# One-hot rows moved from GpSimd to ScalarE and VectorE, gathers queued behind masks, first scalings by ScalarE

## The chip, the cores and the metric

The kernel runs on one core of one Trainium2 chip, in one launch. Its engines work from queues of their own and meet at semaphores: TensorE (PE; its weight loads are shown apart as PEld), VectorE (DVE), ScalarE (ACT), GpSimd (POOL) and SyncE (SP), which issues most DMA transfers. Indirect transfers (gathers by a list of rows) are issued by GpSimd. The metric is the device time of one execution in microseconds, lower is better. [...]

## The reference

Three layers follow one another, all in fp32 at the interface. First a gated linear attention over 4 batches, 8 heads, 768 positions, 48 dimensions per head:

```python
for t in range(S):
    state = alpha[:, :, t, :, None] * state + np.einsum('bhd,bhe->bhde', k[:, :, t], v[:, :, t])
    y[:, :, t] = np.einsum('bhd,bhde->bhe', q[:, :, t], state)
```

Its output, as 3072 tokens of 384 values, goes through a mixture of 8 experts with hidden width 1024. A noisy gate takes the two best experts of each token; each token's two expert outputs are weighted by a softmax of the two logits and added:

```python
top2 = np.argpartition(-noisy_logits, 2, axis=1)[:, :2]
...
h = np.maximum(x[mask] @ w1[e], 0.0)
out[mask] += top2_w[mask, k, None] * (h @ w2[e])
```

Last comes a gated layer of width 1536 on all tokens: `(sigmoid(x @ w_gate) * (x @ w_val)) @ w_out`.

## The kernel before

The products of the experts and of the last layer are made from numbers split in a high and a low part, with three matmuls for each product (lines 521 to 523). The high part is a copy by ScalarE, the low part the difference, by an engine that the caller names (`split`, line 466). For weights that is GpSimd (`wlo`, 128x768 at a time, line 469).

**Attention and router rounds** (about the first 150 us). The attention is done in 24 units: 6 chunks of 128 positions, 4 pairs of heads each. `unit(u, ...)` (line 254) writes the order of all engines by hand: scores of unit u+1 (`st_S`, which ends in ScalarE's copy `am` and GpSimd's mask of it, line 115), then outputs of unit u (`st_Y`, ScalarE's `xt`), state update, transposes (`xr`), the state's scaling (`st`), and the scans of unit u+3 on VectorE (`st_T`), with `d`, a small copy by ScalarE, made one unit ahead (`st_D`). Four slots in a unit, TURN, COUNT, DECIDE and LAST, take other steps. After each chunk the gate routes its 512 tokens in a round: logits, softplus, the two best experts, counts, ranks. Then the round writes its tokens in a table, token number by expert and rank, by matmuls with one-hot rows: `ohl` (128 columns for the low seven bits of the rank, times the token number) as weights and `ohh` (56 columns for expert and the rank's high part) as the moving side, four tiles of 128 tokens for each of the two choices (`router_table`, line 408: `hot`, `mm`, `add`). `hot(0)` stands three units after the round's start, `mm(0)` and `hot(1)` in the next unit, `mm(1)` and `add(1)` in the one after (the list `when`, line 971). Rounds 0 to 3 add up in one PSUM tile; that of chunk 3 ends with a copy to `tab`.

**First expert.** The tokens of chunks 0 to 3 that go to expert 0 are gathered early (`early_fetch`: three gathers `xrow` of 128 rows), transposed and used as the first half of expert 0. The rounds of chunks 4 and 5 are worked off beside that half's matmuls; their order from there on is set by the scheduler of the build, which lays out each engine's queue from its own model of times. `ready` (line 1021) then turns the full table into an index, computes the rows and weights for later, and gathers the second half. An expert half is 8 groups of nine or so matmuls (`ph`, then `h` by ScalarE and VectorE) and a row tile's worth of output matmuls each (`py`).

**Second MoE.** Eight blocks of 384 tokens; for each, two rows of every token are gathered (`grow`), the first scaled by its weight on VectorE (line 850, written with a column of zeros), the second scaled and added (line 852), transposed and run through the gated layer: `sg` (line 878) frees the PSUM tiles, `gh` and `gl` are the split of the result. `gl` is made by GpSimd in block 0, by VectorE in the others.

Of the kernel before, what the change touches and what calls it, by code (L numbers as in the profile page):

```python
# [9 lines left out]
FT = mybir.dt.float32  # L10
# [13 lines left out]
def attention(tc, g):  # L24
# [178 lines left out]
    def round_steps(c):  # L203

        v = {}
        hot, mm, add = router_table(tc, g, c)

        def logits():
            v["ls"] = st_L(c)

        def soft():
            v["lt"] = st_P(v["ls"])
            router_soft(tc, g, v)

        def count():
            router_count(tc, g, c, v)

        def rank():
            router_rank(tc, g, c, v)

        fix = [lambda: router_fix(tc, g, v), lambda: router_lack(tc, g, v)] if c == g.c0 else [lambda: None] * 2
        return [logits, soft, lambda: router_choice(tc, g, c, v), count, rank, *fix,
                lambda: hot(0), lambda: mm(0), lambda: (add(0), hot(1)), lambda: mm(1), lambda: add(1)]

    def fill(k):
        for _ in range(k):
# [53 lines left out]
def router_consts(ctx, tc, g):  # L280
# [16 lines left out]
    nc.vector.tensor_scalar(g.tri, g.iotaP, g.tcol, None, op0=OP.is_gt)  # L297
    g.ones = c.tile([128, 128], BF, name="ones")
    nc.vector.memset(g.ones, 1.0)
    g.noise = c.tile([128, g.NT, E], FT, name="noise")  # L300
    g.load_noise = lambda: nc.sync.dma_start(g.noise, g.nh)

    g.mb = [c.tile([128, B + 1, E], BF, name=f"mb{i}") for i in range(2)]
    nc.vector.memset(g.mb[0][:, B], 0.0)
    g.zero = c.tile([128, 1], FT, name="zero")
    nc.vector.memset(g.zero, 0.0)
    g.roff = c.tile([128, E], FT, name="roff")
    nc.vector.memset(g.roff, 0.0)
    g.wts = c.tile([128, g.NT, 2], FT, name="wts")
# [98 lines left out]
def router_table(tc, g, c):  # L408

    nc, rw = tc.nc, g.rw  # L410
    B = g.B
    T = slice(c * B, (c + 1) * B)
    EN = g.E * g.NB
    v = {}

    def hot(k):
        lo = rw.tile([128, B, 128], FR, name="ohl", tag="ohl", bufs=1)
        for b in range(B):
            n = c * B + b
            nc.gpsimd.tensor_scalar(lo[:, b], g.iotaP, g.low[:, n, k:k + 1], g.ids[:, n:n + 1], op0=OP.is_equal, op1=OP.mult)  # L420
        hi = rw.tile([128, B, EN], FR, name="ohh", tag="ohh", bufs=1)
        cf = g.codes.rearrange("p e a -> p (e a)")[:, None, :].to_broadcast([128, B, EN])
        nc.vector.tensor_tensor(hi, cf, g.code[:, T, k:k + 1].to_broadcast([128, B, EN]), op=OP.is_equal)
        v[k] = lo, hi

    def mm(k):
        lo, hi = v[k]
        own = c > g.c0
        tab = v["tab"] = g.pst("tb", [128, EN]) if own else g.ptab
        for b in range(B):  # L430
            nc.tensor.matmul(tab, lo[:, b], hi[:, b], start=b == 0 and (own or c == k == 0), stop=b == B - 1,
                             skip_group_check=True)

    def add(k):

        if c > g.c0:
            nc.vector.tensor_tensor(g.tab, g.tab, v["tab"], op=OP.add)
        elif c == g.c0 and k == 1:
            nc.vector.tensor_copy(g.tab, g.ptab)

    return hot, mm, add


def router_fix(tc, g, v):
# [378 lines left out]
def moe2(tc, g, out):  # L823
# [11 lines left out]
    def load_x(i):  # L835
# [5 lines left out]
        def fetch():  # L841
            for b in range(TB):
                n = i * TB + b
                ga = []
                for k in range(2):
                    r = g.sx.tile([128, g.DM], FT, name="grow", tag="xrow", bufs=5)
                    g.got = nc.gpsimd.indirect_dma_start(out=r, out_offset=None, in_=src, in_offset=bass.IndirectOffsetOnAxis(  # L847
                        ap=g.row[:, n, k:k + 1], axis=0)).ins
                    ga.append(r)
                nc.vector.scalar_tensor_tensor(ga[0], ga[0], g.wts[:, n, 0:1], g.zero.to_broadcast([128, g.DM]),  # L850
                                               op0=OP.mult, op1=OP.add)
                nc.vector.scalar_tensor_tensor(ga[0], ga[1], g.wts[:, n, 1:2], ga[0], op0=OP.mult, op1=OP.add)
                xs.append(ga[0])
            x["h"] = g.sx.tile([128, KD, NT], FR, name="x2h", tag="xh", bufs=2)
            x["l"] = g.sx.tile([128, KD, NT], FR, name="x2l", tag="xl", bufs=2)
# [9 lines left out]
    def compute(i, x, bg, after, before_last=None):  # L865
        xh, xl = x["h"], x["l"]
        gs = []
        for f in range(FB):
# [9 lines left out]
            nc.vector.tensor_tensor(sg, sg, pp[1], op=OP.mult)  # L878
            hh = g.sh2.tile([128, NT], FR, name="gh", tag="h", bufs=26)
            hl = g.sh2.tile([128, NT], FR, name="gl", tag="h", bufs=26)  # L880
            a, b = split(nc, hh, hl, sg, nc.vector if i else nc.gpsimd)
            gs.append((hh, hl))
            with tc.issue_after(a.ins), tc.issue_after(b.ins):
                bg.step(1)
# [23 lines left out]
def kernel(  # L908
# [14 lines left out]
    g = K()  # L923
# [39 lines left out]
    with tc.tile_pool(name="xrp", bufs=1) as g.xr, tc.tile_pool(name="aconst", bufs=1) as g.ac, \  # L963
# [5 lines left out]
        TURN, COUNT, DECIDE, LAST = range(4)  # L969

        when = [(0, COUNT), (1, TURN), (1, DECIDE), (2, COUNT), (2, DECIDE), (3, COUNT), (3, DECIDE), (3, TURN),
                (4, COUNT), (4, DECIDE), (5, COUNT), (5, DECIDE)]
        soon = when[:5] + [(3, LAST)] * 2 + [(4, LAST)] * 5
        late = []
        for c in range(g.NC - 1):
# [9 lines left out]
            first["steps"][0]()  # L985

        u0 = g.c0 * NP + NP + 5
        plan_a[u0][DECIDE].append(early_fetch)
        for d in range(3):
            plan_a[u0 + 2][COUNT].append(lambda d=d: first["steps"][1 + d]())  # L990
        w0 = expert_steps(g, 0, ahead=True)
# [17 lines left out]
    with tc.tile_pool(name="sh", **tile_wise) as g.sh, tc.tile_pool(name="ps2", space=PSUM, **tile_wise) as g.ps2:  # L1009
# [10 lines left out]

        def ready():
            idx = nxt["idx"] = router_index(tc, g)
            router_rows(tc, g, g.rw)
            overflow_plan(tc, g, plan)
            nxt["steps"], nxt["x"] = expert_x(tc, g, 0, *halves[1], g.sx, idx, g.xd)
            nxt["steps"][0]()

        def behind(f):
            with tc.issue_after(g.last_mask), tc.issue_after(g.last_y):
# [125 lines left out]
```

## Time and profile before

| | us |
|---|---|
| median of 3 runs (1123.96 to 1128.1) | 1124.64 |
| the profiled execution | 1121.54 |
| its span, first to last instruction | 1119.8 |
| TensorE busy | 1074.2 (96%) |
| TensorE's weight loads busy | 1032.1 (92%) |
| VectorE busy | 460.3 (41%) |
| ScalarE busy | 374.1 (33%) |
| GpSimd busy | 372.1 (33%) |

The profile shows one execution. Busy shares over the span are means over stages with different limits: TensorE's idle time lies almost all in the first fifth of the span. In the rows below "idle before" is the time in which an engine stood before an instruction, with the instruction that released it. Matmuls are pipelined, so one that follows another overlaps it.

### The profile page before, as it was taken

The page shows a single profiled execution, that of the slowest core. Times are in us where ns is not written, and L with a number is a line of the kernel's source. Part 1 is how long each engine was busy: PE and PEld are TensorE (multiplying, and loading weights), DVE is VectorE, ACT ScalarE, POOL GpSimd, SP SyncE. Part 2 cuts the span into 40 slices and gives each one's busy share as a digit, 9 for nine tenths or more (in the row PEclk, how much of TensorE's full clock was granted, in tenths as well). Part 3 has the DMA queues.
Part 4 walks back from the last instruction along what each step waited for, and adds up shares of the span by engine and source line. Part 5 has one row for each costly group of instructions (what it writes and reads, how often), then busy time and mean ns, then how long its engine had stood idle before and what let it go on. Part 6 is the DMA issues. An engine that isn't in the chain of part 4 may idle for free. (4 is left out here: it accounts for less than half of the span.)

```text
span 1119.8 us, 18728 instructions
## 1 busy us (share of the span) xinstructions
PE 1074.2 (96%) x7618; PEld 1032.1 (92%) x7618; DVE 460.3 (41%) x940; ACT 374.1 (33%) x801; POOL 372.1 (33%) x310
## 2 busy tenths in 40 slices
PE   7889889799999999999999989999999999999998
PEld 6778769699999999999999989999999999999998
DVE  8989834324544354532222432251414141413131
ACT  4646534223333333333333433131313131313131
POOL 4488878523434232324332745220101010100000
PEclk9989879799999999999999999999999999999999
DMA  8766544425646464645332630210101101000000
GB/s 235 198 177 196 140 130 123 132 72 164 209 139 219 144 194 138 198 143 179 90 101 67 187 91 23 79 43 29 32 33 29 36 27 38 22 23 1 22 1 22
DMA packets 48074, 115.50 MB, mean 103 GB/s; under 512 B 6464, under 2 KB 24800, under 8 KB 47984
## 3 DMA queue, kind: packets, MB, share of 16 engines
q1 hardware_dynamic: 41456, 94.60, 27.9%
q0 software_dynamic: 6528, 19.67, 5.9%
q8 instruction: 61, 1.00, 0.4%
q14 instruction: 29, 0.24, 0.1%
HBM read 87.50 MB, written 26.74 MB: 102 GB/s over the span
## 5 line engine op out<-in xcount | busy, mean ns | idle before, releaser
L469 POOL TENSOR_TENSOR wlo<-raw,whi 128x768 fp32r<-128x768 f32 x82 | 151.7, 1856 | 244.3 <-ACT whi L468 244.2
L521 PE MATMUL pg<-x2h,whi 128*128 128x384 f32 x576 | 195.1, 339 | 2.8 <-DVE sg L878 2.8
L523 PE MATMUL pg<-x2h,wlo 128*128 128x384 f32 x576 | 193.4, 336 | 0.0
L522 PE MATMUL pg<-x2l,whi 128*128 128x384 f32 x576 | 193.2, 335 | 0.0
L586 DVE SCALAR_TENSOR_TENSOR h<-ph,h 128x384 fp32r<-128x384 f32 x192 | 78.6, 443 | 200.3 <-ACT h L583 200.3
L878 DVE TENSOR_TENSOR sg<-sg,pg 128x384 f32<-128x384 f32 x96 | 53.1, 553 | 212.4 <-PE pg L523 199.2
L521 PE MATMUL ph<-xh,whi 128*128 128x384 f32 (+1 forms) x384 | 135.6, 354 | 0.6 <-ACT xh L468 0.6
L522 PE MATMUL ph<-xl,whi 128*128 128x384 f32 (+1 forms) x384 | 135.7, 354 | 0.0
L523 PE MATMUL ph<-xh,wlo 128*128 128x384 f32 (+1 forms) x384 | 135.4, 353 | 0.0
L847 POOL DMA_INDIRECT grow<-yd,row x48 | 46.7, 973 | 263.3 <-PE pt L860 197.4
L521 PE MATMUL py<-whi,h 128*128 128x384 f32 x384 | 133.0, 346 | 0.8 <-ACT yrow L609 0.4
L522 PE MATMUL py<-wlo,h 128*128 128x384 f32 x384 | 128.1, 335 | 0.0
L583 ACT ACTIVATE h<-ph 128x448 fp32r<-128x448 f32 (+1 forms) x128 | 65.4, 516 | 177.4 <-PE ph L523 175.1
L523 PE MATMUL py<-whi,h 128*128 128x384 f32 x384 | 118.3, 337 | 1.2 <-DVE h L586 1.1
L521 PEld LDWEIGHTS pg<-x2h,whi 128*128 128x128 f32 x576 | 108.7, 189 | 3.3 <-DVE sg L878 3.1
L522 PEld LDWEIGHTS pg<-x2l,whi 128*128 128x128 f32 x576 | 108.7, 189 | 0.0
L523 PEld LDWEIGHTS pg<-x2h,wlo 128*128 128x128 f32 x576 | 108.6, 189 | 0.0
L521 PE MATMUL po<-whi,gh 128*128 128x384 f32 x288 | 96.3, 334 | 2.1 <-issue 2.1
L468 ACT ACTIVATE gh<-sg 128x384 fp32r<-128x384 f32 x96 | 50.3, 524 | 142.1 <-DVE sg L878 142.0
L523 PE MATMUL po<-whi,gl 128*128 128x384 f32 x288 | 96.2, 334 | 0.0
L522 PE MATMUL po<-wlo,gh 128*128 128x384 f32 x288 | 96.2, 334 | 0.0
L468 ACT ACTIVATE whi<-raw 128x768 fp32r<-128x768 f32 x82 | 68.9, 844 | 67.0 <-DMA raw<-in_w2h_dram 50.6
(169 smaller groups left out, 1770.4 us busy)
## 6 DMA issues: line engine op xcount, KB each, us to landing
ur<-in_uh_dram SPq DMA_DIRECT2D x23, 675.5 KB, 5.6
raw<-in_w1h_dram SPq DMA_DIRECT2D x32, 384.0 KB, 3.6
raw<-in_w2h_dram SPq DMA_DIRECT2D x32, 384.0 KB, 3.9
yd<-yrow SPq DMA_DIRECT2D x48, 192.0 KB, 2.1
w<-t SPq DMA_DIRECT2D x36, 192.0 KB, 2.0
raw<-w SPq DMA_DIRECT2D x18, 384.0 KB, 3.2
xv<-in_vh_dram SPq DMA_DIRECT2D x6, 768.0 KB, 9.0
xd<-xr SPq DMA_DIRECT2D x6, 768.0 KB, 6.1
```

Of the source, the lines that this page charges most:

```text
L468: a = nc.scalar.activation(hi, src, AF.Copy)
L469: b = e.tensor_tensor(lo, src, hi.bitcast(FT), op=OP.subtract)
L521: nc.tensor.matmul(out, wh, mh, start=first, stop=False)
L522: nc.tensor.matmul(out, wh, ml, start=False, stop=False)
L523: nc.tensor.matmul(out, wl, mh, start=False, stop=last)
L583: a = nc.scalar.activation(h[:, :tot], p[:, :tot], AF.Relu)
L586: b = nc.vector.scalar_tensor_tensor(h[:, lo:lo + j - i], p[:, i:j], 0.0, h[:, i:j].bitcast(FT), op0=OP.max, op1=OP.subtract)
L847: g.got = nc.gpsimd.indirect_dma_start(out=r, out_offset=None, in_=src, in_offset=bass.IndirectOffsetOnAxis(ap=g.row[:, n, k:k + 1], axis= ...
L878: nc.vector.tensor_tensor(sg, sg, pp[1], op=OP.mult)
```

## The change

It has five parts.

1. `hot` is split. For the first choice of rounds 0 to 3, ScalarE makes `ohl` tile by tile in two instructions: |low - column|, and then max(0, id - id x that), which is the token number where they agree and 0 elsewhere. The four tiles stand in four slots of one unit. Everywhere else (`hot`) VectorE makes all four tiles of `ohl` in one comparison, without the token number, and ScalarE multiplies the four tiles of `ohh` by it. GpSimd makes none.
2. `early_fetch` moves from the end of one unit to the TURN slot of the next, behind that unit's masks.
3. `ready` gathers directly after the index.
4. The first scaling of gathered rows is ScalarE's in blocks 0 and 1, and a form without the zeros on VectorE in the others.
5. `gl` of block 0 is VectorE's.

```diff
--- before.py
+++ after.py
@@ -203,7 +203,7 @@
     def round_steps(c):
 
         v = {}
-        hot, mm, add = router_table(tc, g, c)
+        hot, part, mm, add = router_table(tc, g, c)
 
         def logits():
             v["ls"] = st_L(c)
@@ -220,7 +220,8 @@
 
         fix = [lambda: router_fix(tc, g, v), lambda: router_lack(tc, g, v)] if c == g.c0 else [lambda: None] * 2
         return [logits, soft, lambda: router_choice(tc, g, c, v), count, rank, *fix,
-                lambda: hot(0), lambda: mm(0), lambda: (add(0), hot(1)), lambda: mm(1), lambda: add(1)]
+                *([lambda b=b: part(0, b) for b in range(B)] if c <= g.c0 else [lambda: hot(0)]),
+                lambda: mm(0), lambda: (add(0), hot(1)), lambda: mm(1), lambda: add(1)]
 
     def fill(k):
         for _ in range(k):
@@ -297,13 +298,13 @@
     nc.vector.tensor_scalar(g.tri, g.iotaP, g.tcol, None, op0=OP.is_gt)
     g.ones = c.tile([128, 128], BF, name="ones")
     nc.vector.memset(g.ones, 1.0)
+    g.nids = c.tile([128, g.NT], FT, name="nids")
+    nc.vector.tensor_scalar(g.nids, g.ids, -1.0, None, op0=OP.mult)
     g.noise = c.tile([128, g.NT, E], FT, name="noise")
     g.load_noise = lambda: nc.sync.dma_start(g.noise, g.nh)
 
     g.mb = [c.tile([128, B + 1, E], BF, name=f"mb{i}") for i in range(2)]
     nc.vector.memset(g.mb[0][:, B], 0.0)
-    g.zero = c.tile([128, 1], FT, name="zero")
-    nc.vector.memset(g.zero, 0.0)
     g.roff = c.tile([128, E], FT, name="roff")
     nc.vector.memset(g.roff, 0.0)
     g.wts = c.tile([128, g.NT, 2], FT, name="wts")
@@ -413,15 +414,29 @@
     EN = g.E * g.NB
     v = {}
 
-    def hot(k):
+    def tiles(k):
         lo = rw.tile([128, B, 128], FR, name="ohl", tag="ohl", bufs=1)
-        for b in range(B):
-            n = c * B + b
-            nc.gpsimd.tensor_scalar(lo[:, b], g.iotaP, g.low[:, n, k:k + 1], g.ids[:, n:n + 1], op0=OP.is_equal, op1=OP.mult)
         hi = rw.tile([128, B, EN], FR, name="ohh", tag="ohh", bufs=1)
         cf = g.codes.rearrange("p e a -> p (e a)")[:, None, :].to_broadcast([128, B, EN])
         nc.vector.tensor_tensor(hi, cf, g.code[:, T, k:k + 1].to_broadcast([128, B, EN]), op=OP.is_equal)
         v[k] = lo, hi
+
+    def hot(k):
+
+        tiles(k)
+        lo, hi = v[k]
+        nc.vector.tensor_tensor(lo, g.iotaP[:, None, :].to_broadcast([128, B, 128]),
+                                g.low[:, T, k:k + 1].to_broadcast([128, B, 128]), op=OP.is_equal)
+        for b in range(B):
+            nc.scalar.activation(hi[:, b], hi[:, b].bitcast(FT), AF.Copy, scale=g.ids[:, c * B + b:c * B + b + 1])
+
+    def hot_part(k, b):
+
+        if b == 0:
+            tiles(k)
+        lo, n = v[k][0], c * B + b
+        nc.scalar.activation(lo[:, b], g.iotaP, AF.Abs, bias=g.low[:, n, k:k + 1], scale=-1.0)
+        nc.scalar.activation(lo[:, b], lo[:, b].bitcast(FT), AF.Relu, bias=g.ids[:, n:n + 1], scale=g.nids[:, n:n + 1])
 
     def mm(k):
         lo, hi = v[k]
@@ -438,7 +453,7 @@
         elif c == g.c0 and k == 1:
             nc.vector.tensor_copy(g.tab, g.ptab)
 
-    return hot, mm, add
+    return hot, hot_part, mm, add
 
 
 def router_fix(tc, g, v):
@@ -847,8 +862,10 @@
                     g.got = nc.gpsimd.indirect_dma_start(out=r, out_offset=None, in_=src, in_offset=bass.IndirectOffsetOnAxis(
                         ap=g.row[:, n, k:k + 1], axis=0)).ins
                     ga.append(r)
-                nc.vector.scalar_tensor_tensor(ga[0], ga[0], g.wts[:, n, 0:1], g.zero.to_broadcast([128, g.DM]),
-                                               op0=OP.mult, op1=OP.add)
+                if i < 2:
+                    nc.scalar.activation(ga[0], ga[0], AF.Copy, scale=g.wts[:, n, 0:1])
+                else:
+                    nc.vector.tensor_scalar(ga[0], ga[0], g.wts[:, n, 0:1], None, op0=OP.mult)
                 nc.vector.scalar_tensor_tensor(ga[0], ga[1], g.wts[:, n, 1:2], ga[0], op0=OP.mult, op1=OP.add)
                 xs.append(ga[0])
             x["h"] = g.sx.tile([128, KD, NT], FR, name="x2h", tag="xh", bufs=2)
@@ -878,7 +895,7 @@
             nc.vector.tensor_tensor(sg, sg, pp[1], op=OP.mult)
             hh = g.sh2.tile([128, NT], FR, name="gh", tag="h", bufs=26)
             hl = g.sh2.tile([128, NT], FR, name="gl", tag="h", bufs=26)
-            a, b = split(nc, hh, hl, sg, nc.vector if i else nc.gpsimd)
+            a, b = split(nc, hh, hl, sg, nc.vector)
             gs.append((hh, hl))
             with tc.issue_after(a.ins), tc.issue_after(b.ins):
                 bg.step(1)
@@ -969,7 +986,7 @@
         TURN, COUNT, DECIDE, LAST = range(4)
 
         when = [(0, COUNT), (1, TURN), (1, DECIDE), (2, COUNT), (2, DECIDE), (3, COUNT), (3, DECIDE), (3, TURN),
-                (4, COUNT), (4, DECIDE), (5, COUNT), (5, DECIDE)]
+                (3, COUNT), (3, DECIDE), (3, LAST), (4, COUNT), (4, DECIDE), (5, COUNT), (5, DECIDE)]
         soon = when[:5] + [(3, LAST)] * 2 + [(4, LAST)] * 5
         late = []
         for c in range(g.NC - 1):
@@ -985,7 +1002,7 @@
             first["steps"][0]()
 
         u0 = g.c0 * NP + NP + 5
-        plan_a[u0][DECIDE].append(early_fetch)
+        plan_a[u0 + 1][TURN].append(early_fetch)
         for d in range(3):
             plan_a[u0 + 2][COUNT].append(lambda d=d: first["steps"][1 + d]())
         w0 = expert_steps(g, 0, ahead=True)
@@ -1020,10 +1037,10 @@
 
         def ready():
             idx = nxt["idx"] = router_index(tc, g)
+            nxt["steps"], nxt["x"] = expert_x(tc, g, 0, *halves[1], g.sx, idx, g.xd)
+            nxt["steps"][0]()
             router_rows(tc, g, g.rw)
             overflow_plan(tc, g, plan)
-            nxt["steps"], nxt["x"] = expert_x(tc, g, 0, *halves[1], g.sx, idx, g.xd)
-            nxt["steps"][0]()
 
         def behind(f):
             with tc.issue_after(g.last_mask), tc.issue_after(g.last_y):
```

How the queues change, at three places. On ScalarE, in the unit three after a chunk's end (the first such unit). `am`, `xt`, `km`, `xr`, `st` and `d` are the copies of the attention. Before:

```order
L114 ACTIVATE am<-sc 128x512 x2
L146 ACTIVATE xt<-y 128x512
L125 ACTIVATE km<-tr 128x448
L182 ACTIVATE xr<-tr 128x4x96
L173 ACTIVATE st_141<-uu,pd 112x48 x4
L77 ACTIVATE d_136<-ur_132 112x4
```

Now:

```order
L114 ACTIVATE am<-sc 128x512 x2
L438 ACTIVATE ohl<-iotaP,low 128x128
L439 ACTIVATE ohl<-ohl,ids,nids 128x128
L146 ACTIVATE xt<-y 128x512
L125 ACTIVATE km<-tr 128x448
L182 ACTIVATE xr<-tr 128x4x96
L438 ACTIVATE ohl<-iotaP,low 128x128
L439 ACTIVATE ohl<-ohl,ids,nids 128x128
L173 ACTIVATE st_141<-uu,pd 112x48 x4
L77 ACTIVATE d_136<-ur_132 112x4
```

Two tiles of `ohl` stand in this unit between `am` and `st`, each as two instructions; two more follow after `d`.

On GpSimd, from the last units of the attention to the second gather of the first expert. `xrow` are the gathers, `am` the masks, `wlo` the low halves of weights; two pieces of `ohl` and of `wlo` are left out in the middle of the first fence. Before:

```order
L115 AFFINE_SELECT am<-am 128x512 x2
L546 DMA xrow<-xd,idx 128x384 x3
L115 AFFINE_SELECT am<-am 128x512 x2
L420 TENSOR_SCALAR ohl<-iotaP,low,ids 128x128 x4
L469 TENSOR_TENSOR wlo<-raw,whi 128x768 x3
...
L420 TENSOR_SCALAR ohl<-iotaP,low,ids 128x128 x4
L469 TENSOR_TENSOR wlo<-raw,whi 128x768 x3
L546 DMA xrow<-xd,idx 128x384 x3
L546 DMA xrow<-xd,idx 64x384
L546 DMA xrow<-xd,idx 128x384
```

Now:

```order
L484 TENSOR_TENSOR wlo<-raw,whi 128x768
L115 AFFINE_SELECT am<-am 128x512 x10
L561 DMA xrow<-xd,idx 128x384 x3
L484 TENSOR_TENSOR wlo<-raw,whi 128x768 x8
L561 DMA xrow<-xd,idx 128x384 x3
L561 DMA xrow<-xd,idx 64x384
L561 DMA xrow<-xd,idx 128x384
L484 TENSOR_TENSOR wlo<-raw,whi 128x768 x3
```

The three early gathers stand behind the last two masks instead of ahead of them, and the one-hot rows are gone. The second gather stands behind eight `wlo` of this stage instead of eleven.

On TensorE, at the end of the first half of expert 0. `tb<-ohh,ohl` are the table matmuls of the last round's second choice, `py` the expert's output matmuls, `pt<-ident,xrow` the transposes of the second gather. Before:

```order
L521 MATMUL py_2880<-whi_2633,h_2709 128x384
L522 MATMUL py_2880<-wlo_2634,h_2709 128x384
L523 MATMUL py_2880<-whi_2633,h_2709 128x384
L431 MATMUL tb_2716<-ohh_2697,ohl_2692 128x56 x4
L662 LDWEIGHTS ones_79
L662 MATMUL tb_2734<-mb0_82,ones_79 128x8
L556 MATMUL pt_2821<-ident_59,xrow_2773 128x128
L556 MATMUL pt_2828<-ident_59,xrow_2773 128x128
```

Now:

```order
L446 MATMUL tb_2740<-ohh_2716,ohl_2715 128x56 x3
L538 MATMUL py_2807<-whi_2655,h_2694 128x384
L538 MATMUL py_2859<-whi_2655,h_2694 128x384
L446 MATMUL tb_2740<-ohh_2716,ohl_2715 128x56
L536 MATMUL py_2807<-whi_2655,h_2733 128x384
L537 MATMUL py_2807<-wlo_2656,h_2733 128x384
L536 MATMUL py_2859<-whi_2655,h_2733 128x384
L537 MATMUL py_2859<-wlo_2656,h_2733 128x384
L538 MATMUL py_2807<-whi_2655,h_2733 128x384
L538 MATMUL py_2859<-whi_2655,h_2733 128x384
L677 LDWEIGHTS ones_79
L677 MATMUL tb_2768<-mb0_84,ones_79 128x8
```

The table matmuls stood behind all `py` of the half; now six `py` stand between them and the last count, and 24 more between that and the transposes.

## Rows read from the trace of the kernel before

**Rows 1.** Busy time, instructions and clock of each engine in three stretches

```profile
core 0: us, PE busy (x) PEld busy (x) DVE busy (x) ACT busy (x) POOL busy (x), PEclk, DMA share, GB/s
0.00:150.00 150.00, 129.15 (x2232) 113.95 (x2234) 130.35 (x256) 81.31 (x239) 102.20 (x98) 0.92 0.67 190
150.00:216.00 66.00, 52.19 (x332) 45.64 (x327) 25.94 (x96) 22.90 (x45) 47.69 (x42) 0.82 0.43 128
216.00:1119.00 903.00, 892.91 (x5061) 872.54 (x5060) 303.99 (x588) 269.84 (x518) 222.23 (x170) 1.00 0.28 87
```

**Rows 2.** TensorE's waits, 0 to 216 us

```profile
PE wm L431 <- POOL ohl L420: 10.7, 9, 2.1
...
PE y L143 <- POOL am L115: 3.7, 2, 2.9
```

**Rows 3.** VectorE's waits, 40 to 150 us

```profile
DVE pd L93 <- ACT d L77: 7.1, 5, 2.0
DVE tab L439 <- PE wm L431: 4.0, 1, 4.0
```

**Rows 4.** GpSimd's groups by shape, 0 to 216 us

```profile
L420 POOL TENSOR_SCALAR ohl<-iotaP,low,ids 128x128 fp32r<-128x128 f32 x48 | 60.9, 1276 | 9.6 <-DVE low L390 4.9 <-PE tb L431 4.6
```

**Rows 5.** ScalarE's groups by shape, 0 to 150 us

```profile
L173 ACT ACTIVATE st<-uu,pd 112x48 f32<-112x48 f32 x80 | 17.6, 316 | 0.0
...
L195 ACT ACTIVATE ls<-tr 128x128 f32<-128x128 f32 x5 | 1.4, 278 | 17.4 <-PE tr L192 17.4
```

**Rows 6.** ScalarE's groups by shape, 640 us to the end

```profile
L468 ACT ACTIVATE gh<-sg 128x384 fp32r<-128x384 f32 x96 | 50.3, 524 | 142.1 <-DVE sg L878 142.0
```

**Rows 7.** VectorE in order of time: start, duration, instruction [idle before]

```profile
112.50 0.68 DVE L99 TENSOR_TENSOR qt<-ur,pd 112x512 f32<-112x512 f32 x1
...
116.51 1.12 DVE L99 TENSOR_TENSOR qt<-ur,pd 112x512 f32<-112x512 f32 x1
...
144.09 0.38 DVE L423 TENSOR_TENSOR ohh<-codes,code 128x224 fp32r<-128x224 f32 x1
...
148.48 0.22 DVE L439 COPY tab<-wm 128x56 f32<-128x56 f32 x1 [4.01 <-PE wm L431]
```

**Rows 8.** TensorE in order of time, end of the first expert's first half

```profile
193.80 0.52 PE L431 MATMUL tb<-ohh,ohl 128*128 128x56 f32 x4
...
204.65 1.09 PE L556 MATMUL pt<-ident,xrow 128*128 128x128 f32 x4 [1.29 <-DMA xrow<-xd,idx]
206.33 1.12 PE L521 MATMUL ph<-xh,whi 128*128 128x448 f32 x2 [0.59 <-ACT xh L468]
```

**Rows 9.** TensorE in order of time, around the first gather

```profile
156.07 2.55 PE L143 MATMUL y<-am,xv 128*64 128x128 f32 x16 [2.90 <-POOL am L115]
...
159.45 0.85 PE L556 MATMUL tr<-ident,xrow 128*128 128x128 f32 x3
...
166.04 0.44 PE L521 MATMUL ph<-xh,whi 128*128 128x384 f32 x1
```

**Rows 10.** GpSimd in order of time, around both gathers

```profile
154.41 0.94 POOL L546 DMA_INDIRECT xrow<-xd,idx  x1 [0.30 <-issue]
...
192.67 5.34 POOL L469 TENSOR_TENSOR wlo<-raw,whi 128x768 fp32r<-128x768 f32 x3
...
198.17 1.05 POOL L546 DMA_INDIRECT xrow<-xd,idx  x1 [0.16 <-DVE ofr L657]
```

**Rows 11.** Indirect DMA issues, 0 to 216 us, with median us to landing

```profile
xrow<-xd,idx POOLq DMA_INDIRECT x12, 3.1
```

**Rows 12.** VectorE in order of time, the cast of the index

```profile
194.61 1.69 DVE L462 CAST idx<-tab 128x56 int32<-128x56 f32 x1
```

**Rows 13.** VectorE's groups by shape, 640 us to the end

```profile
L469 DVE TENSOR_TENSOR gl<-sg,gh 128x384 fp32r<-128x384 f32 x84 | 46.7, 556 | 34.9 <-ACT gh L468 34.9
```

**Rows 14.** TensorE in order of time, block 0 of the second MoE

```profile
666.26 0.44 PE L521 MATMUL pg<-x2h,whi 128*128 128x384 f32 x1 [2.83 <-DVE sg L878]
```

**Rows 15.** VectorE in order of time, block 0 of the second MoE

```profile
662.15 3.59 DVE L850 SCALAR_TENSOR_TENSOR grow<-grow,wts,zero 128x384 f32<-128x384 f32 x1 [0.56 <-DMA grow<-yd,row]
```

## The prediction

> **What bounds the kernel now.** I read the busy times by stretch first, because the mean over the whole run hides three stages. From 216 us to the end TensorE is busy 892.9 of 903 us at full clock: 5061 matmuls, 0.176 us each [rows 1]. Nothing that makes another engine faster there can shorten it by more than the few idle microseconds. Between 0 and 216 us it is busy 181.3 of 216, at mean granted clocks of 0.92 and 0.82 [rows 1]. That is where time can be had: the attention with its router rounds (to about 150 us) and the first expert (150 to 216 us).
>
> The second view is what TensorE waits for in this stretch: 10.7 us in nine waits for `ohl`, the one-hot rows that GpSimd makes, and 3.7 us for `am`, the masks that GpSimd makes too [rows 2]. The third is what VectorE, the engine with most work in the attention (130.4 of 150 us [rows 1]), waits for: 7.1 us in five waits for ScalarE's `d`, and 4.0 us once for the table matmul [rows 3]. The `d` waits are the echo of the first: TensorE stands at `ohl`, ScalarE's evacuations stand behind TensorE, `d` is queued behind these, and VectorE's next scan needs `d`. Last I read three places in order of time: TensorE and GpSimd at the two gathers of the first expert, and TensorE and VectorE at the one long wait of the second MoE; their rows stand with the parts below.
>
> **Part 1: one-hot rows leave GpSimd.** Removed there: 48 instructions of 1276 ns, 60.9 us [rows 4]; GpSimd was busy 149.9 of 216 us [rows 1]. Added:
> - ScalarE, first choice, rounds 0 to 3: eight instructions of 128x128 a round. The nearest row is `ls`, also 128x128, 278 ns; the bounds are 316 ns (`st`, only 48 columns but with a scale per partition, spread over pipelined neighbours) and 524 ns (`gh`, 384 columns) [rows 5, 6]. I take 0.3: 2.4 us a round. Second choice: four scalings of 56 columns at the price of `st`, 1.3 us. That is 3.7 us a round on an engine that is idle 68.7 of 150 us [rows 1]; were this idle time not where it is wanted, it would cost the whole 3.7.
> - VectorE, second choice: one comparison of 128x512 with two SBUF inputs. `qt` has this form: 0.68 us alone, 1.12 beside the masks [rows 7]. I take 0.7 and keep 1.12; four of them make 2.8 (up to 4.5) us.
>
> In the attention I take VectorE as the bound of the changed kernel, since its idle time is what is left once TensorE's waits go. Gain: the 7.1 us of `d` waits, less 2.8 for the comparisons. Then the last table: `ohh` is compared at 144.09 for 0.38 us and `tab` follows only at 148.48 [rows 7]. In the new form the row comparison (0.7) and ScalarE's scalings (1.3) run side by side after `ohh`, then the matmul (0.5 [rows 8]); 1.8 to 2 us instead of 4.0. Another 2.0. Sum of part 1: 6.3 us, with VectorE late next.
>
> **Part 2: gathers behind masks.** Before, three gathers stand ahead of the last unit's masks on GpSimd, and TensorE waits 2.90 us for `am` at 156.07 [rows 9]. The last gather starts at 154.41 [rows 10] and lands 3.1 us after its issue [rows 11], so at 157.5; but TensorE takes the rows only at 159.45 because it is late from the masks. With masks first and no one-hot rows in between, the gathers still start with the index (GpSimd has nothing else then), and TensorE waits for the rows instead of for the masks: 159.45 - 157.5 = 1.9 us. What is queued behind the gathers on GpSimd is `wlo` of the second weights, which have 72 matmuls of time. ScalarE's new wait for `ohh` of round 4 stands ahead of the last `xt`; the transposes of that `xt` come after the gathered rows, so the rows' landing covers it.
>
> **Part 3: the second gather of the first expert.** Before, the last table matmul (193.80 + 0.52) is the end of the first half's work; then index (194.61 + 1.69 [rows 12]), gather at 198.17 behind three `wlo` that end at 198.01 [rows 10], the last awaited row at 204.65, first matmul at 206.33 [rows 8]. From 194.32 to 206.33 are 12.0 us without expert work. The order of the changed kernel puts 30 matmuls of `py` behind the last table matmul (6, the count, 24) and the gather ahead of the three `wlo`. The chain is then 12.0 less the queueing of 198.17 - 196.30 = 1.9, so 10.1; 30 x 0.176 = 5.3 of it are covered; 4.8 remain. Gain 7.2 us. Two conditions: GpSimd must have finished the eight `wlo` ahead of the gather (without 48 one-hot instructions between them I count it done), and the two choices of the last round must follow each other within the 21 matmuls (3.7 us) that lie between their tables: table sum 0.2 (like `tab` [rows 7]), `ohh` 0.4, then 1.3 for the scalings, 1.9 in all.
>
> **Part 4: second MoE.** The low halves `gl` of block 0 go to VectorE, 12 at 0.556 us [rows 13], and the first scalings of two blocks to ScalarE, 6 at 0.524 [rows 6]. TensorE's pace is 18 matmuls, 3.2 us, for one `gl`, so both are covered. The one wait of TensorE there, 2.83 us at 666.26 for `sg` [rows 14], came from a scaling on VectorE that took 3.59 us at 662.15 [rows 15] in front of it. That instruction is gone, and GpSimd is down to gathers and `wlo`: gain 2.8. The later scalings on VectorE (blocks 2 to 7) lie beside a full TensorE: 0. The constants (`nids` for `zero`): 0.
>
> [...] The row: the index cast, seven columns for each of eight experts, took 1.69 us while GpSimd ran `wlo` [rows 10, 12]; `ohh`, four times as wide, took 0.38 alone [rows 7]. [...]
>
> **Sum.** 6.3 + 1.9 + 7.2 + 2.8 = 18.2 us. The profiled execution took 1121.5 us (its span 1119.8), so 1103.3; the median of the runs, 1124.6, is 3.1 above it, and on that basis I forecast 1106.4 us.
>
> **Rivals.**
> - VectorE takes the attention's gain back: each comparison 1.12, and the table as late as now: 7.1 - 4.5 = 2.6 instead of 6.3, so 1110. For it: VectorE is the busiest engine there. Against it: the masks, which slow it, keep their number. 0.13.
> - The tables of the last round come late, and TensorE waits ahead of its 30 matmuls instead of behind them. A hold of 1.3 (1.69 less 0.38) on each of two comparisons and a ScalarE busy with `h` would bring the 1.9 us above the 3.7; the loss is between 0.8 and all of 5.3, I take 3.5: 1110. For it: `wlo` runs without a break there. 0.17.
> - VectorE is held by `wlo` in block 0: `gl` is 0.556 + 1.3, and with `sg` and a sum of rows this is above the pace of 3.2 in three of twelve steps. The 2.8 are lost and some 2 more: 1111. 0.10.
> - Several of these at once, 12 us: 1118. 0.06.
> - Slower: ScalarE takes its instructions in order, so the first `ohl` of a round, which needs `low` from VectorE, holds `xt`, `st` and `d` behind it if VectorE is late. If VectorE is a unit behind (130.4 / 24 = 5.4 us) in each of four rounds, 21.7 are lost and the 6.3 too: 1124.6 - 18.2 + 28 = 1134. It decides from 18.2 / 4 = 4.6 us a round. Against it: before, VectorE waits for ScalarE's `d` and not the other way [rows 3]. 0.04.
>
> **How the numbers follow.** The forecast has 0.50. Its own ends: the index not held and full clock after shorter waits give 3 to 6 us more, a comparison at 1.12 gives 2 us less: 1100 to 1109. The range for 8 in 10 takes in the rivals up to 1115 and 1097 below. No change means within 0.5%, about what a measurement can tell here, so 1119 to 1130: 0.05, half of the 1118 case and a little of each single one. Slower 0.04, faster 0.91.
>
> **What would show it.** Right: no wait of TensorE for one-hot rows in the attention; `tab` near 142 us; transposes of the gathered rows at about 151, the second half's first `ph` near 191, no 2.8 us wait for `sg` in block 0; from there to the end the same TensorE time. Wrong: waits of TensorE for `ohh` or `ohl` of some microseconds a round, ScalarE waiting for `low`, a table matmul with idle time ahead of the last 30 `py`, or `wlo` still ahead of the gather.

## The result and the profile after

Measured: 1105.7 us, median of four runs (1103.9 to 1107.0), against 1124.3 (1123.6 to 1128.1) for the kernel before on the same chip; ratio 0.983, 95% interval 0.980 to 0.985. The forecast was 1106.4. The profiled execution took 1106.3 us, its span 1104.5.

The stretches first, in the columns of [rows 1] (PEclk is TensorE's granted clock, a share of the full one):

```profile
0.00:150.00 150.00, 128.99 (x2296) 112.48 (x2296) 137.29 (x279) 98.27 (x294) 61.33 (x71) 0.97 0.67 192
150.00:216.00 66.00, 60.06 (x335) 53.63 (x335) 25.85 (x91) 27.05 (x59) 33.83 (x25) 0.90 0.43 128
216.00:1104.00 888.00, 879.52 (x4991) 860.17 (x4989) 301.85 (x585) 270.06 (x518) 207.90 (x155) 1.00 0.28 88
```

GpSimd's first 150 us fell from 102.2 busy us [rows 1] to 61.3, ScalarE's rose to 98.3, VectorE's to 137.3 of 150. From 216 us to the end are 888 us in place of 903.

What TensorE waits for up to 216 us, answering [rows 2]:

```profile
PE y L138 <- ACT xt L146: 5.2, 4, 1.5
PE tr L192 <- ACT km L125: 4.1, 4, 1.3
PE sc L112 <- DVE qt L99: 3.7, 2, 3.5
PE tr L571 <- DMA xrow<-xd,idx: 2.5, 3, 1.0
```

What VectorE waits for between 40 and 150 us, answering [rows 3]; and one of ScalarE's waits up to 150 us:

```profile
DVE tab L454 <- PE wm L446: 1.6, 1, 1.6
```

```profile
ACT ohl L438 <- DVE low L391: 13.7, 4, 3.8
```

TensorE's waits for GpSimd's `ohl` are gone, and VectorE waits for no `d`. New are four waits of ScalarE for `low`, 3.3 to 3.8 us each: its first `ohl` of a round stands in its queue before VectorE has `low`. Behind it stand `xt` and `km` (one `xt` started at 107.33, its `y` ready at 103.88), and TensorE waits for these.

VectorE at the last of the four tables, answering [rows 7], then TensorE at the two starts of the first expert and the last table matmul, answering [rows 8, 9], and GpSimd at the second gather, answering [rows 10]:

```profile
140.10 0.38 DVE L421 TENSOR_TENSOR ohh<-codes,code 128x224 fp32r<-128x224 f32 x1
140.41 0.68 DVE L428 TENSOR_TENSOR ohl<-iotaP,low 128x512 fp32r<-128x512 f32 x1
142.67 0.22 DVE L454 COPY tab<-wm 128x56 f32<-128x56 f32 x1 [1.59 <-PE wm L446]
...
181.62 0.21 DVE L452 TENSOR_TENSOR tab<-tab,tb 128x56 f32<-128x56 f32 x1 [0.69 <-PE tb L446]
```

```profile
158.44 0.69 PE L536 MATMUL ph<-xh,whi 128*128 128x384 f32 x1
158.92 0.52 PE L537 MATMUL ph<-xl,whi 128*128 128x384 f32 x1
...
181.39 0.19 PE L446 MATMUL tb<-ohh,ohl 128*128 128x56 f32 x1
...
191.34 1.11 PE L536 MATMUL ph<-xh,whi 128*128 128x448 f32 x2 [0.63 <-ACT xh L483]
```

```profile
181.16 1.83 POOL L484 TENSOR_TENSOR wlo<-raw,whi 128x768 fp32r<-128x768 f32 x1 [3.85 <-ACT whi L483]
183.31 0.96 POOL L561 DMA_INDIRECT xrow<-xd,idx  x1 [0.32 <-DVE oov L672]
...
189.27 5.38 POOL L484 TENSOR_TENSOR wlo<-raw,whi 128x768 fp32r<-128x768 f32 x3
```

Read as milestones of the two profiled executions (us; the gain so far beside what the prediction's terms add up to there):

| | before | after | gain | predicted |
|---|---|---|---|---|
| table of rounds 0 to 3 copied | 148.48 | 142.67 | 5.8 | 6.3 |
| first matmul, first half | 166.04 | 158.44 | 7.6 | 8.2 |
| last table added | 194.36 | 181.62 | 12.7 | 13.5 |
| first matmul, second half | 206.33 | 191.34 | 15.0 | 15.4 |
| first output row out of PSUM | 702.0 | 684.9 | 17.1 | 18.2 |
| end of the span | 1119.8 | 1104.5 | 15.3 | 18.2 |

The medians differ by 18.6: the first profiled execution lay 2.8 below its median, the second 0.6 above its own. Gain is lost again behind 158, 191 and 685 us; these places are looked at below, and the greater part at each is the granted clock, 0.50 there for 2 to 7 us.

### The profile page after: what moved, and what is told of

Its sections match the earlier page's. It is cut to its first block, busy times and chain, and to the rows that moved or that the text cites. A ratio compares the mean times of both kernels' runs of the same rounds, so it can differ in the third digit from the quotient of the medians.

```text
span 1104.5 us, 18735 instructions
## 1 busy us (share of the span) xinstructions
PE 1068.6 (97%) x7618; PEld 1026.3 (93%) x7618; DVE 465.0 (42%) x954; ACT 395.4 (36%) x871; POOL 303.1 (27%) x250
```

## The experiments

Each ratio is to the kernel before on the same chip, five rounds, with its 95% interval. Single executions of one kernel differ by up to 14 us, so a ratio can't tell 2 us; there the traces decide, each of one execution.

### The parts by themselves

`only_rows` is the kernel before with the one-hot rows of the diff alone.

> The kernel before with the one-hot rows of the change alone (first choice by ScalarE in parts, second by one comparison of VectorE); the two fetches, the low halves and the scalings of block 0 as before. Theory by steps: this edit carries the whole of part 1 (6.3 us) and the larger half of part 3, because the 30 matmuls of py move behind the last table matmul with it alone (5.3 us): 11.6 us off, 1124.3 - 11.6 = 1112.7, ratio 0.990. Rival: the second fetch and the masks carry the rest, and this edit gives only the 6.3 of the attention: 1118, ratio 0.9945; the matmuls that stand behind the table would then only be time spent waiting earlier. In the trace: table near 142.7 in both cases; first matmul of the second half near 196 by the theory, 199 or later by the rival.

`no_rows` is its complement.

> The changed kernel with the one-hot rows back on GpSimd as before; all the other edits stay. Theory by steps: what is left is part 2 (1.9), the queueing ahead of the second gather (1.9) and block 0 (2.8): 6.6 us off 1124.3, so 1117.7, ratio 0.994. Rival: the parts are not additive, since with 48 one-hot instructions on GpSimd the early gathers again stand among its work and the masks gain nothing: only 2.8 remain, 1121.5, ratio 0.9975.

Measured: only_rows 0.988 (0.984 to 0.993), 13.3 us off 1127.3; no_rows 0.994 (0.991 to 0.996), 7.0 off. The sum, 20.3, is that of the whole change (19.4 from its ratio) within the intervals, which are wide (8 to 18 us for only_rows, 4 to 10 for no_rows). GpSimd at the second gather, in only_rows and then in no_rows:

```profile
183.68 1.83 POOL L486 TENSOR_TENSOR wlo<-raw,whi 128x768 fp32r<-128x768 f32 x1 [3.86 <-ACT whi L485]
185.83 0.96 POOL L563 DMA_INDIRECT xrow<-xd,idx  x1 [0.32 <-DVE oov L674]
...
191.79 5.35 POOL L486 TENSOR_TENSOR wlo<-raw,whi 128x768 fp32r<-128x768 f32 x3
```

```profile
192.96 5.35 POOL L469 TENSOR_TENSOR wlo<-raw,whi 128x768 fp32r<-128x768 f32 x3
198.45 1.05 POOL L546 DMA_INDIRECT xrow<-xd,idx  x1 [0.15 <-DVE ofr L657]
```

This corrects the expectations of both runs. I had put the 1.9 us of queueing behind three `wlo` to the lines moved in `ready`. But only_rows, where these lines stand as before, has the gather ahead of the three `wlo`; and no_rows, where they are moved, still has it behind. From the addition of the last table to this gather it is 1.7 us in only_rows and in the change, 3.8 in the kernel before and 3.9 in no_rows, so the moved lines are worth nothing. The one-hot rows bring all of part 3: only_rows should have gained 6.3 + 5.3 + 1.9 = 13.5 and no_rows 4.7. The measured 13.3 and 7.0 agree, but their intervals take in the 11.6 and 6.6 expected too; the traces decide. In that of only_rows the second half starts at 194.06, 12.3 us earlier than in the kernel before: about 1.1 less than the sum, and its first half starts 1.1 later behind its table (18.7 us; before 17.6).

Part 2 is seen in no_rows: from its table (150.26) to the first `ph` (165.68) are 15.4 us, in the kernel before 17.6 (table of [rows 7], first `ph` of [rows 9]): 2.1 us, predicted 1.9. At the second half's start 0.9 of it is left (56.9 us behind the table, before 57.9).

### Block 0 of the second MoE

```
- split(nc, hh, hl, sg, nc.vector)
+ split(nc, hh, hl, sg, nc.vector if i else nc.gpsimd)
- first scalings: ScalarE (i < 2), VectorE tensor_scalar (later)
+ nc.vector.scalar_tensor_tensor(ga[0], ga[0], wts, g.zero, ...)
```

> The changed kernel with only part 4 undone: low halves of block 0 by GpSimd, all first scalings by VectorE in the form with the zero operand. Theory by steps: the wait of 2.8 us for sg in block 0 comes back, 1105.7 + 2.8 = 1108.5, ratio to the changed kernel 1.0025. Rival: the wait is not what that scaling causes, since a wait of 1.0 for sg is still there after the change with VectorE held at gl instead: then only 1.8 or nothing comes back, 1105.7 to 1107.5.

Measured 0.983 (0.978 to 0.987), like the changed kernel: inconclusive. Its trace says more: the second half starts at 191.45 (after 191.34), and the first output row comes at 687.9 (684.9), 3.0 later. VectorE and TensorE there, in no_block0:

```profile
649.44 3.62 DVE L867 SCALAR_TENSOR_TENSOR grow<-grow,wts,zero 128x384 f32<-128x384 f32 x1 [0.51 <-issue]
```

```profile
PE pg L538 <- DVE sg L895: 2.8, 1, 2.8
```

The same scaling is held again (3.62 us, [rows 15] 3.59, the one before it 0.62) and the same wait returns. In the changed kernel another instruction is held in its place, and TensorE's wait for `sg` is 1.0:

```profile
PE pg L536 <- DVE sg L895: 1.0, 1, 1.0
```

```profile
652.63 3.40 DVE L484 TENSOR_TENSOR gl<-sg,gh 128x384 fp32r<-128x384 f32 x1 [0.59 <-ACT gh L483]
```

```profile
651.96 3.64 POOL L484 TENSOR_TENSOR wlo<-raw,whi 128x768 fp32r<-128x768 f32 x2
```

So the size is the rival's, 1.8, not the 2.8 of the theory. From the last `py` to the first output row no_block0 takes 48.4 us, the changed kernel 46.5: 1.9, the two waits' difference. The other 1.1 of the 3.0 are lost ahead of that `py`, where waits for `h` take 1.6 us in no_block0 and 0.3 in the changed kernel. The kernel before takes 49.8 there, since its wait was followed by half the clock (granted clock 0.5 from 667.6 to 671.0 us, a loss of 1.7); in no_block0 the clock stayed at 1.00.

### What sets a round's length: ScalarE's hold, or VectorE

`late_parts` takes ScalarE's steps out of the way of `xt` and `km`:

```
- (3, TURN), (3, COUNT), (3, DECIDE), (3, LAST), (4, COUNT), ...
+ (3, LAST), (3, LAST), (3, LAST), (3, LAST), (4, COUNT), ...
```

> The changed kernel with the four ScalarE steps for the first choice all at the end of the third unit of a round, behind its xt, km, xr, st and d. ScalarE's waits for low (13.7 us in four) should go in any case, and TensorE's waits for xt and km (5.2 and 4.1 us) with them. Theory: VectorE is the bound of the attention, since it waits for no d any more and is busy 137.3 of 150 us; so TensorE's time is only spent elsewhere, and the table comes within 0.7 us of 142.7: 1105 to 1106.5. Rival: ScalarE's hold is what sets the pace of a round; then 2 x 1.3 us a round come back, up to 10 us, so 1096 to 1100 and the table near 133 to 137.

Measured 0.976 (0.972 to 0.980), table at 137.83, the middle round of three (one `ohh` to the same one of the next round) 23.06 us in place of 24.76. That is between the two: more than my theory (a table within 0.7 of 142.7), a little less than the rival (near 133 to 137). As it was another chip than the changed kernel's, both were run again side by side.

> The changed kernel as it is, to stand beside late_parts on one chip; against the kernel before it should again be near 0.983 (0.980 to 0.985). Open is whether the four late ScalarE steps gain anything: late_parts was at 0.976 (0.972 to 0.980) on another chip. Theory: they take 1.7 us a round from four rounds and so 5 to 7 us of the run: 0.978 to 0.983 here for this one and 0.005 to 0.006 less for late_parts. Rival: single executions scatter by 4 us either way, and the difference of the two is under 2 us.

> The kernel late_parts once more, beside the changed kernel on the same chip. Theory: 5 to 7 us faster than the changed kernel, a round of 23.06 us in place of 24.76 in its trace. Rival: within 2 us of the changed kernel; then where the first-choice steps stand matters less than the start of the loads and the places at which the clock is halved.

Measured 0.979 (0.975 to 0.983) for the changed kernel and 0.981 (0.977 to 0.985) for late_again. ScalarE's waits are gone (`ohl` for `low` 13.2 us in four in after_again, 0.2 in late_again), the table comes at 138.93 against 141.05, the second half starts at 186.97 against 188.86, and the run is no faster. From the second half's start to the end of the span late_again takes 917.1 us, after_again 912.2. Most of these 4.9 us are waits that its trace shows; VectorE and TensorE in an expert:

```profile
444.63 0.82 DVE L527 SCALAR_TENSOR_TENSOR t<-raw,mask 128x384 int32<-128x384 int32 x1 [1.62 <-DMA raw<-in_wvh_dram]
...
446.55 1.28 DVE L601 SCALAR_TENSOR_TENSOR h<-ph,h 128x384 fp32r<-128x384 f32 x4
```

```profile
447.16 0.61 PE L538 MATMUL py<-whi,h 128*128 128x384 f32 x2 [2.17 <-DVE h L601]
```

VectorE, in order, stands before a weight that has not landed, with four `h` behind it, and TensorE waits 2.17 us for one. TensorE's waits for `h` between 190 and 560 us are 5.5 us here, 1.1 in after_again, 1.8 in late_parts. The first late run lacked them, so whether they belong to the edit or to the execution stays open; that late_parts is faster than the change is not shown.

Why the middle round is 1.7 us shorter is shown. VectorE is without long gaps in both: its 47 records of that round add up to 25.05 us in the changed kernel and 23.47 in late_parts (neighbours overlap a little), and 1.07 and 1.06 us of the round lie under no record. The same instructions are shorter: the cast of `ei` 1.25 before and 0.46 now, one `gi` scan 1.67 and 1.34, one of two long `qt` 1.12 and 0.68. GpSimd's masks and `wlo` in a round are as many as before; the instructions stand at other moments of them. The cast of `ei` ran beside a `wlo` in the changed kernel and ended with it (97.58 + 1.82 = 99.40, and 98.19 + 1.25 = 99.44):

```profile
98.19 1.25 DVE L347 CAST ei<-i 128x8 f32<-128x8 uint32 x1
```

```profile
97.58 1.82 POOL L484 TENSOR_TENSOR wlo<-raw,whi 128x768 fp32r<-128x768 f32 x1 [2.47 <-ACT whi L483]
```

`late_vector` and `late_all_scalar` price VectorE from both sides, `double_mask` the masks:

```
late_vector:      first choice by hot(0), in all rounds
late_all_scalar:  second choice by part(1, b) in rounds 0 to 3
double_mask:      each affine_select of am twice
```

> The kernel late_parts with the first choice of rounds 0 to 3 made like the second: one comparison of 128x512 more on VectorE a round, and four scalings of ohh on ScalarE in place of eight instructions of 128x128. Theory: VectorE runs without a gap in the attention and sets a round's length (23.06 us in late_parts), so a round gets longer by the 0.68 us of that comparison, to 23.7, and the table comes near 140.5: about 1102, ratio to before 0.979. Rival: ScalarE, which takes its work in order, sets it: it is relieved of 2.2 us a round (8 x 0.40 less 4 x 0.26), a round gets 1 to 2 us shorter, 1091 to 1096.

> The kernel late_parts with the second choice of rounds 0 to 3 made like the first, by eight ScalarE instructions: the comparison of 0.68 us leaves VectorE, 2.2 us a round come to ScalarE. Theory (VectorE sets the round): 22.4 us a round in place of 23.06, table near 135.1, about 1097, ratio 0.974. Rival (ScalarE sets it, busy 20.5 of 25 us before this): a round of 24 us or more, 1103 or more.

> The kernel late_parts with each mask on GpSimd applied twice (the second changes nothing in the data); nothing is added on VectorE. Theory: the difference between the changed kernel (24.76 us a round) and late_parts (23.06) lies in how long VectorE's own two-input operations are held beside masks (1.5 of the 1.7 us: kt 0.87 to 0.94 in place of 0.69, qt 1.12 in place of 0.68, the cast of ei 1.25 in place of 0.46). Twice the masks then make VectorE's same operations longer by 1 to 2.7 us a round: table near 143 to 148, 1105 to 1110, with VectorE still without gaps. Rival: VectorE's durations don't depend on GpSimd and the masks only lengthen the chain to TensorE by 1.0 us each: VectorE's operations keep their lengths, and gaps behind d appear on it.

| | ratio | middle round, us | VectorE's records in it | under no record |
|---|---|---|---|---|
| late_parts | 0.976 (0.972 to 0.980) | 23.06 | 23.47 | 1.06 |
| double_mask | 0.992 (0.990 to 0.995) | 26.71 | 27.10 | 1.11 |
| late_vector | 0.985 (0.983 to 0.987) | 25.52 | 24.86 | 2.16 |
| late_all_scalar | 0.983 (0.981 to 0.986) | 25.34 | 24.28 | 2.30 |

VectorE in double_mask, where nothing was added on it:

```profile
106.08 1.43 DVE L348 CAST ei<-i 128x8 f32<-128x8 uint32 x1
...
108.73 1.70 DVE L93 TENSOR_TENSOR_SCAN pd<-ur,d 112x512 f32<-112x512 f32 x1
...
112.83 1.12 DVE L99 TENSOR_TENSOR qt<-ur,pd 112x512 f32<-112x512 f32 x1
```

double_mask bears out the theory, beyond its expected size: the round is 3.65 us longer, VectorE's own instructions by 3.63, with no new gap. Of this 0.97 is the cast (1.43, in late_parts 0.46); 2.66 lie in other instructions, with eight more masks on GpSimd in the round. Not only masks count: the cast of `ei` in the changed kernel ended with a `wlo`, and the `gl` above only behind the two `wlo` beside it, at 656.03 (652.63 + 3.40), these at 655.60 (651.96 + 3.64). What makes VectorE wait there is not shown.

late_vector misses both theories. A comparison more on VectorE costs 2.5 us in the middle round, not 0.68: 1.4 in its records, 1.1 in a new gap (1.1 and 1.4 in the rounds beside it, without a gap). late_all_scalar, with a comparison less, comes out as its rival had it: the round is 2.3 longer (25.34; "24 us or more"), the median 1106.3 ("1103 or more"), and VectorE now waits for ScalarE, 3.9 us in five waits for `d` and 2.4 in four for `ex` of the softplus between 20 and 150 us. There ScalarE takes its part in a round's length; but VectorE's records are longer as well, though one fewer. VectorE in late_vector:

```profile
100.07 1.23 DVE L93 TENSOR_TENSOR_SCAN pd<-ur,d 112x512 f32<-112x512 f32 x1 [1.07 <-ACT d L77]
...
101.55 2.45 DVE L95 TENSOR_TENSOR_SCAN gi<-ur,d 112x512 f32<-112x512 f32 x1
```

The longest scan, 1.23 with GpSimd idle (at 83.44 in the changed kernel), now stands beside the `wlo` of 100.85 to 102.91 and the masks from 102.88 on, where in late_parts GpSimd's `wlo` ran beside the small search instructions; and a wait for `d` is back. So in the changed kernel and in late_parts VectorE sets a round's length, ScalarE is not far behind it, and moving one instruction shifts what stands beside what, which can be worth more than the instruction.

### The clock behind a gap

`fill_both`, `fill_small` and `fill_small_second` put useless matmuls into the gaps ahead of the first expert's halves, on top of late_parts:

```
+ g.fill(6)   # 3 in fill_small, 0 in fill_small_second: ahead of each
              # transpose of d == 0 in the first half's turn
+ for _ in range(14):   # 5 in the two others: behind the last table
+     tc.nc.tensor.matmul(wm, g.ident, idx (as f32), start=True, stop=True)
```

> The kernel late_parts with matmuls of no use in the two gaps ahead of the first expert's halves: six of 128x128 ahead of each of the first three transposes of gathered rows, and fourteen of 56 columns behind the last table. Theory: part of what a shorter gap gains is given back, because the stretch at granted clock 0.5 (149.5 to 155 and 186 to 192 in late_parts) starts after the gap and falls on useful matmuls, at 0.32 us each in place of 0.176; without the idle time it does not come, and some 2 to 2.5 us at each place are gained: 1095 to 1097, ratio 0.972. [...]

> The kernel fill_both with fewer idle matmuls: three of 128x128 ahead of each of the first three transposes of gathered rows (0.75 us each, the waits there are 0.7 to 1.0), five of 56 columns behind the last table (1.2 us, the gaps there are 0.4, 0.5, 0.3 and 0.6). In fill_both the granted clock never fell below 1.0 between 140 and 210 us, but the filling itself held the transposes up by 1 and 3 us. Theory: with the excess gone, what the clock gives stays: about 1.5 us ahead of the first half and 2 ahead of the second, so 3 us less than late_parts, ratio to before 0.973. Rival: with so little filling the half-rate stretches come back, and the time is that of late_parts, 0.976, or the useless matmuls cost as much as the clock gives.

> The kernel late_parts with the five idle matmuls behind the last table alone, none in the first gap. Theory: the half-rate stretch of 186 to 192 us goes, worth about 2 us; that of 149.5 to 155 stays: 1 to 2 us less than late_parts and 1 to 2 more than fill_small, first matmul of the second half 48 to 48.5 us behind the table as in late_parts, and full clock behind it. Rival: the second stretch stays too, and the time is that of late_parts.

Measured: 0.981 (0.978 to 0.984), 0.983 (0.980 to 0.986), 0.984 (0.981 to 0.987); none is faster than late_parts or the change. TensorE around the second half's start by stretch, columns as above, first the kernel before, then after, then fill_small:

```profile
206.00:210.00 4.00, 3.67 (x11) 2.82 (x12) 1.78 (x3) 1.25 (x3) 1.78 (x3) 0.50 0.44 116
210.00:214.00 4.00, 4.00 (x24) 3.66 (x23) 0.87 (x3) 1.45 (x4) 2.04 (x3) 0.97 0.58 162
```

```profile
190.00:194.00 4.00, 3.36 (x12) 2.34 (x13) 1.16 (x2) 1.52 (x3) 4.00 (x3) 0.66 0.70 197
194.00:198.00 4.00, 4.00 (x13) 3.46 (x12) 0.62 (x1) 0.84 (x1) 3.23 (x4) 0.50 0.81 235
198.00:202.00 4.00, 3.77 (x21) 3.21 (x20) 1.28 (x4) 0.98 (x2) 3.07 (x3) 0.99 0.51 153
```

```profile
186.00:190.00 4.00, 2.92 (x14) 1.94 (x15) 1.33 (x3) 1.91 (x4) 4.00 (x3) 1.00 0.59 162
190.00:194.00 4.00, 3.77 (x21) 3.14 (x20) 1.35 (x4) 1.83 (x3) 3.23 (x4) 1.00 0.84 260
```

Before, the granted clock is 0.5 when the first `ph` comes at 206.33, and stays so until 210.2 (0.97 is a half rate of 0.24 of the next 4 us): 3.9 us. After, the gap is shorter, the clock falls only at its end (0.66 is 2.7 of 4 us, from 191.3 on), and the half rate lasts until 198.1, 6.7 us of useful matmuls: 13 matmuls in four us in place of 24. At half rate half the time is lost, 3.4 against 1.9: 1.4 of the 15.0 us are given back. The filling does keep the clock: at 1.00 in the fill_small stretch above, and at both gaps in fill_both (146 to 200 us), where late_parts has 0.50 from 150 to 154 and from 186 to 192. So at these places the half rate came with the gap, and with the gap filled it did not come. But in fill_both it also made the transposes late (first `ph` 10.8 us behind the last table, late_parts 9.5), and fill_small's 10.0 eats part of what is left. Worth a microsecond or two at most, which these intervals don't show.

## Why the prediction was right

- **Bound.** Right: all the gain lies ahead of 216 us but for block 0, and the milestones of the traces follow the terms within 1 us up to the second half's start.
- **Part 1**, 6.3: measured 5.8. Three rounds (`ohh` to `ohh`) went from 78.8 to 74.3 us, 4.6 gained where 7.1 - 2.8 was put; the comparison took 0.68, as good as the 0.7 assumed. From the last round's first `ohh` to the table 2.1 was gained, 1.8 of it behind the second `ohh` (4.4 to 2.6 us), where 2.0 was predicted. The first `ohh` came 0.9 later in the second execution. The words "VectorE late next" held in the form that VectorE has no gaps; that where its instructions stand beside masks and `wlo` is worth 1.6 us a round and more I had seen only in one `qt`. The `qt` and the `ohh` of [rows 7] that the prediction calls alone stood beside GpSimd's `ohl` (108.94 to 116.40, 143.62 to 147.46); with GpSimd idle the changed kernel has the same 0.68 (at 110.07) and 0.38 (at 140.10). ScalarE's new instructions cost 0.40 and 0.49, not 0.3; no gap of VectorE in a round came of it.
- **Part 2**, 1.9: 1.8 in the change (7.6 less 5.8), 2.1 in no_rows; about 1.1 of it is given back, since the first `ph` come at half rate (0.32 us from one to the next from 158.92 on) until 160.6 and before they did not.
- **Part 3**, 7.2: right in the sum (15.0 less 7.6 is 7.4, although the 1.1 just named falls into this stretch: some 1 us more than forecast was gained in it, and where is open) and in its mechanism; the attribution, made only in the expectations, to the moved lines of `ready` was wrong.
- **Part 4**, 2.8: right in its cause, too large by the 1.0 of the wait for `sg` that is left: 1.9 by no_block0. That wait comes from the held `gl`, as the rival on block 0 had it, though it was held for 2.8 us (3.40 less the 0.556 of [rows 13]) and not for the 1.3, an estimate of mine from one cast. What made up for it was luck: before, the wait was followed by half the clock, 1.7 more, so 3.3 were gained there (49.8 to 46.5). (The cast of [rows 12] has one input, `qt`, `gl` and the scaling of [rows 15] have two; which forms are held is not shown.)
- **Rivals.** ScalarE's wait for `low`, given 0.04, was there in each of the four rounds, at 3.3 to 3.8 us. It was also among the prediction's own signs of being wrong. It stayed under the 4.6 that I had worked out as deciding, and taking it away gave no time that the second pair of runs could measure. The case against it ("VectorE waits for `d` and not the other way") was poor: the waits of the kernel before say nothing of a wait that a new instruction brings. VectorE did not take the gain back: each comparison in the attention took 0.68, not 1.12. Late last-round tables did not happen: TensorE waits for none of their rows.
- **The end.** 18.2 by the sum, 15.3 by the spans. Of the 2.9 between them 0.4 is missing at the second half's start; 1.2 are lost on balance from there to the last `py` (638.42; before 652.17), where the 1.4 above falls; 0.5 more than forecast is gained in block 0; and 1.8 are lost behind the first output row. The changed kernel's clock there, in the same columns:

```profile
698.00:700.00 2.00, 1.03 (x5) 1.03 (x6) 0.00 (x0) 0.20 (x1) 1.69 (x2) 0.96 0.26 52
700.00:702.00 2.00, 2.00 (x8) 2.00 (x8) 0.56 (x1) 0.29 (x1) 1.39 (x3) 0.50 0.66 214
702.00:704.00 2.00, 2.00 (x10) 2.00 (x9) 0.62 (x1) 0.49 (x1) 1.64 (x2) 0.68 0.70 190
```

  Behind a gap of 2.1 us at the end of the first block some 3.4 us run at half rate, a loss of 1.7. Before, the same gap is there without it, and the half rate came behind the wait of [rows 14]. The agreement of forecast and median to 0.7 us is therefore partly luck: the forecast lacked terms of this size on both sides, and the two profiled executions stand 2.8 below and 0.6 above their medians.

## What to carry to other kernels

When work leaves GpSimd, count also what VectorE's instructions cost beside what stays on it (here `qt` 1.12 us beside masks, 0.68 without; the cast of `ei` 1.25 beside a `wlo`, 0.17 without); the place of such an instruction was worth more than three times its length in one round here (2.5 us for a comparison of 0.68). Time gained from a wait was partly lost here at the next gap and the next half-clock stretch (1.4 us behind 191, 1.7 behind 700): follow a gain through milestones to the end of the span. And where a program orders the instructions, look at the order with each part of a change alone before saying which line moved what.

## What the runs showed of the hardware that I had not expected

- With eight more masks on GpSimd in a round (1.04 us each in the changed kernel) VectorE's instructions took 2.66 us more without the cast, 0.33 for a mask; beside a `wlo` of 2.06 us and the mask behind it a scan took 2.45 in late_vector (1.23 at 83.44 in the changed kernel, with GpSimd idle), and beside one of 1.82 the cast of `ei` took 1.25 in the changed kernel (0.17 at 98.35 in late_vector, with GpSimd idle).
- A wait of 2 to 3 us in an otherwise full stretch cost up to 1.7 us more here: the granted clock fell to 0.5 for about 3.4 us behind the wait of 2.8 us at 666 us before [rows 14] and behind the gap of 2.1 us at 699 us after. But it stayed at 1.00 behind the same wait in no_block0, and behind the same gap before and in no_rows; in only_rows it fell behind both. What decides between these is not shown.
